# One decay table for all chunks, early loads in idle tiles, joined masks and a written-out order in a fused retention, spectral and gated MLP kernel

## The chip, the cores and the metric

The kernel runs on one core of one Trainium2 chip. The metric is the device time of one execution in microseconds (us). The kernel before takes 381.7 us, the median of 3 runs (381.68 to 381.8).

## The reference

Three stages follow one another. B is 2, there are 8 heads of 64 features, 768 tokens, and the model has 512 features; all data are float32.

```python
# 1: retention, a state per head that decays by gamma at every token
state = gamma * state + outer(k[t], v[t]);  y[t] = q[t] @ state / sqrt(64)
# 2: spectral mixing over tokens
theta = x @ w_theta
zr, zi = x * cos(theta), x * sin(theta)
u = x + w_tok_r @ zr + w_tok_i @ zi          # 768 x 768 over the tokens
x = u + relu(u @ w_ch)
# 3: gated MLP
h = gelu(x @ w_in);  hu, hv = halves of h
v_s = w_sg @ (layernorm(hv) * g_ln) + b_sg    # again over the tokens
out = x + (hu * v_s) @ w_out
```

## The kernel before

Each batch entry is cut into 6 chunks of 128 tokens, 12 chunks i in all. For a chunk, `retention(i)` (L432 on) loads q and k (`load_qk`, 512 KB), k and v (`load_kv`, 512 KB) and a table of q's decays (L485, 256 KB). TensorE then makes the scores, eight 64x128 products into two PSUM banks (`scores`). VectorE multiplies each bank by the causal mask (`mask`, L457, two instructions). ScalarE or VectorE scales v by its decay (`fade_v_heads`, eight instructions of L475, for the first 8 chunks; `fade_v`, L468, for the rest). TensorE makes k times v (`outer`), VectorE adds that to the state (`grow`, L507 and L509), and `attend` adds the state's part and the masked part into one bank. VectorE multiplies the result by the q decays into x (L554). Decays are counted from the start of the sequence, so each of the 6 chunk positions has a table of its own and the state itself is never scaled.

x lives in three tiles: `xa[0]`, `xa[1]` (the first four chunks of each batch entry) and `xb` (the last two of both). `theta(i)` multiplies x by w_theta, takes sine and cosine on ScalarE, turns x by four transposes with `ident` (L648) and multiplies (L656). `mix_main` and `mix_rest` do the token mixing. Then `channels`, `up_v`, `norm`, `up_u`, `gate_tile` and `finish` do the rest in 512-wide tiles.

Every wide product is exact to float32 by three passes of a two-part split: `split_hi` (L310, ScalarE) rounds a tile to float32r, `split_lo` (L316, VectorE) takes the remainder, and `terms3` (L290) issues high by high, low by high and high by low. The weights come packed in 64-bit words, 1 MB for each 128x1024 weight. `weight` loads one into a raw tile, unpacks it by L369 (ScalarE), L378 and L389 twice (VectorE), and splits it. There are two raw tiles (`RAWS`), so the third weight's load waits for the first's split.

The program is a list of operations, each for one engine with what it reads and writes (`Plan.op`). `Plan.schedule` gives them an order and buffers by estimated durations, due times (`prio`) and a look-ahead. The instructions stand on each engine in that order; what they wait for is found from the regions that they read and write. TensorE is kept busy before its data are there: eight products on a zeroed state (`warm`), and `keep_warm`, 128x128 products of `ident` with itself, which the schedule puts into gaps until a planned time of 34 us.

Of the kernel before, what the change touches and what calls it, by code (L numbers as in the profile page):

```python
# [18 lines left out]
P = 128  # L19
NCH = S // P  # L20
NP = H // 2
TA, TB = 512, 256
N = B * NCH

# [36 lines left out]
class Plan:  # L61
# [3 lines left out]
    BEGIN = {"PE": 5.2, "ACT": 2.0, "DVE": 2.0, "POOL": 1.3, "SP": 0.7}  # L65
# [28 lines left out]
    def schedule(self, look):  # L94


        engines = {o.eng: self.BEGIN.get(o.eng, 0.0) for o in self.ops}

        free = {of: [0.0] * n for of, n in self.room.items()}
        rank, level = {}, {}  # L100
        for k, o in enumerate(self.ops):
            o.missing, o.out = len(o.deps), []
            level[o] = max([o.lev, *(level[d] for d in o.deps)])
            rank[o] = k
            for d in o.deps:
                d.out.append(o)
        for o in self.ops:

            if o.eng == "SP" and o.out and not o.deps:
                level[o] = min(level[x] for x in o.out)  # L110
        for k, o in enumerate(sorted(self.ops, key=lambda o: (level[o], rank[o]))):
            o.pos = k
        use = {of: np.zeros(len(self.ops) + 1, np.int64) for of in self.room}
        for b in {b for o in self.ops for b in o.bufs}:
            b.todo = sorted(u.pos for u in b.users)
            b.first = b.todo[0]
            use[b.of][b.first : b.todo[-1] + 1] += 1
        for of, u in use.items():
            assert u.max() <= self.room[of], f"{of}: {u.max()} at {int(u.argmax())}"
        ready = {e: [] for e in engines}  # L120
        for o in self.ops:
            if not o.missing:
                ready[o.eng].append(o)
        state = {"port": 0.0, "dma": 2.1, "first": 0}
        done = [False] * (len(self.ops) + 1)

        def earliest(o):
            t = max(engines[o.eng], o.at, o.prio - (C["PA"] if o.eng == "PE" else C["AHEAD"]))
            if o.port:
                t = max(t, state["port"])  # L130
            o.spots = []
            more = {}
            for b in o.bufs:
                if b.base is not None:
                    continue
                n = more[b.of] = more.get(b.of, 0) + 1
                if b.first > state["first"]:
                    if use[b.of][state["first"] : b.first].max() + n > self.room[b.of]:
                        return None
                spots = sorted((x, k) for k, x in enumerate(free[b.of]) if x is not None)  # L140
                if len(spots) < n:
                    return None
                o.spots.append((b, spots[n - 1][1]))
                t = max(t, spots[n - 1][0] + self.LAT)
            return t

        for e in ready:
            for o in ready[e]:
                o.at = 0.0
        order = []  # L150
        while len(order) < len(self.ops):
            pick = None
            for e, ops in ready.items():
                at = [(t, o) for o in ops if (t := earliest(o)) is not None]
                if not at:
                    continue
                first = min(t for t, _ in at)
                t, o = min(
                    ((t, o) for t, o in at if t <= first + look.get(e, 0.0)),
                    key=lambda x: (x[1].until is not None, x[1].prio, x[0]),  # L160
                )
                if pick is None or t < pick[0]:
                    pick = (t, o)
            if pick is None:
                held = {e: len(v) for e, v in ready.items()}
                raise RuntimeError(f"no room: {len(order)} of {len(self.ops)}, {held}")
            t, o = pick
            earliest(o)
            if o.until is not None and t > o.until:
                o.dur, o.fn = 0.0, lambda: None  # L170
            ready[o.eng].remove(o)
            for b, b.base in o.spots:
                free[b.of][b.base] = None
                use[b.of][: b.first] += 1
            o.start = t
            engines[o.eng] = t + (0.45 if o.eng == "SP" else o.dur)
            if o.eng == "SP":
                state["dma"] = max(state["dma"], t + 0.45) + o.dur
                o.end = state["dma"] + 2.0
            else:  # L180
                o.end = t + o.dur
            if o.port:
                state["port"] = o.end
            done[o.pos] = True
            while done[state["first"]]:
                state["first"] += 1
            for b in o.bufs:
                last = b.todo[-1]
                b.todo.remove(o.pos)
                now = b.todo[-1] if b.todo else -1  # L190
                use[b.of][now + 1 : last + 1] -= 1
                if not b.todo:
                    free[b.of][b.base] = max(u.end for u in b.users)
            for x in o.out:
                x.missing -= 1
                if not x.missing:
                    x.at = max(d.end + (self.LAT if d.eng != x.eng else 0.0) for d in x.deps)
                    ready[x.eng].append(x)
            order.append(o)

        rank = {o: k for k, o in enumerate(order)}
        return sorted(order, key=lambda o: (o.start, rank[o]))


C = dict(TC=13, LATE=90, AHEAD=60, LM=28, LT=9, LR=16, LW=15, LRW=15, PEL=0.1, DVEL=0.1, ACTL=0.7, CHP=5, SGP=10, RW2=0, PA=25, DEL=6, RS=3.8, LEAD=40, TH=-8, WARM=34.0, NWARM=90, FA=8, LEAD1=5)
# [3 lines left out]
def retention_spectral_gmlp(  # L209
# [5 lines left out]
    dqs: bass.AP,  # L215
# [9 lines left out]
    nc.scalar.preload_act_table_set("silu_and_others")  # L225
# [16 lines left out]
    def bank():  # L242
        return Buf("psum")

    def halves(dtype=F32):
        b = Buf("pair", dtype)
# [59 lines left out]
    def dma(kb, fn, **k):  # L306
        return plan.op("SP", kb / 410.0, fn, **k)
# [799 lines left out]
    def keep_warm():  # L1107
# [3 lines left out]
        def products():  # L1111
            mm(ap(t)[:, 0:P], ident, ident, True, True)
# [87 lines left out]
```

## Time and profile before

| what | value |
|---|---|
| median of 3 runs | 381.7 us |
| the profiled execution: its span, first to last instruction | 381.1 us |
| TensorE busy | 374.7 us (98%), 2422 records |
| VectorE busy | 274.0 us (72%) |
| ScalarE busy | 175.0 us (46%) |
| GpSimd busy | 4.3 us (1%) |
| DMA | 41.96 MB, a mean of 110 GB/s |

The profiled execution is told by its span; the 0.6 us by which the median of the runs is longer lie around the first and the last instruction. The page's section on the chain of work that ended last puts 93% of the span on TensorE and 5% on the loads of q, k and v. A product of two float32 tiles leaves two matmul records in the trace, one of float32r tiles leaves one, so eight products of `scores` are "x16".

### The profile page before, as it was taken

Reading aid. Unit: us, or ns where it says so; the run is one execution under the profiler, and the core shown is the slowest. Engines: PE = TensorE matmul, PEld = TensorE weight load, DVE = VectorE, ACT = ScalarE, POOL = GpSimd, SP = SyncE. Lnnn points to the kernel's source line nnn. Section 1 sums busy time; section 2 is a strip of 40 time slices with the busy share of each in tenths; the row PEclk is TensorE's granted clock in tenths of the full one; section 3 lists DMA queues with packets and bytes.
Section 4 is the critical chain, followed back from the end, with each engine's and each line's share of the span. In section 5 each row is a group of like instructions: output and inputs, shape, how many; then the busy total and the mean of one; then the engine's idle time right before and its main releaser. Section 6 shows DMA issues by size and latency. Waiting matters only on the chain.

```text
span 381.1 us, 5873 instructions
## 1 busy us (share of the span) xinstructions
PE 374.7 (98%) x2422; PEld 318.4 (84%) x2422; DVE 274.0 (72%) x408; ACT 175.0 (46%) x292; POOL 4.3 (1%) x10
## 2 busy tenths in 40 slices
PE   7999999999999999999999999999999999999996
PEld 7877888878988978788998888888888888998885
DVE  1798999997977597869816685899899864544222
ACT  3677988563345335465313443595775711110000
POOL 1000000000000000003000000000000000000000
PEclk9999999999999999999999999999999999999999
DMA  7999553453435603029000160000000000000223
GB/s 258 411 407 407 208 191 110 144 223 132 165 114 192 248 2 113 0 101 352 4 2 2 31 244 2 1 0 0 2 0 1 2 1 0 2 2 35 103 89 106
DMA packets 11931, 41.96 MB, mean 110 GB/s; under 512 B 1536, under 2 KB 2560, under 8 KB 9472
## 3 DMA queue, kind: packets, MB, share of 16 engines
q1 hardware_dynamic: 11904, 41.58, 29.5%
q8 instruction: 19, 0.31, 0.3%
q14 instruction: 8, 0.07, 0.0%
HBM read 38.43 MB, written 3.15 MB: 109 GB/s over the span
## 4 chain that ended last, share of the span: by engine, by line
PE 93%; DMA 5%; SPq 0%; DVE 0%; issue 0%
PE b L290 92%; DMA b<-qkv 5%; PE b L648 1%; DVE b L1027 0%; SPq L424 0%; SPq L441 0%; SPq L413 0%
## 5 line engine op out<-in xcount | busy, mean ns | idle before, releaser
L290 PE MATMUL b<-b,b 128*128 128x512 f32 (+2 forms) x1788 | 332.6, 352 | 0.0
L290 PEld LDWEIGHTS b<-b,b 128*128 128x128 f32 (+1 forms) x1788 | 277.5, 183 | 47.0 <-issue 2.4
L310 ACT ACTIVATE b<-b 128x1024 fp32r<-128x1024 f32 (+1 forms) x64 | 53.2, 859 | 66.7 <-DVE b L975 38.2
L316 DVE TENSOR_TENSOR b<-b,b 128x1024 fp32r<-128x1024 f32 (+1 forms) x64 | 59.3, 955 | 9.7 <-ACT b L310 9.5
L389 DVE SCALAR_TENSOR_TENSOR b<-b 128x1024 int32<-128x1024 int32 x38 | 46.5, 1224 | 1.5 <-ACT b L369 0.5
L310 ACT ACTIVATE b<-xa 128x512 fp32r<-128x512 f32 x24 | 14.6, 626 | 22.9 <-DVE xa L777 9.9
L369 ACT ACTIVATE b<-b 128x1024 f32<-128x1024 f32 x19 | 21.8, 1155 | 3.6 <-DMA b<-wts 3.6
L290 PEld LDWEIGHTS b<-b 64*128 64x128 f32 (+1 forms) x352 | 17.3, 164 | 7.0 <-issue 2.8
L290 PE MATMUL b<-b 64*128 64x128 f32 (+1 forms) x352 | 20.5, 258 | 2.1 <-DMA b<-qkv 2.1
L457 DVE TENSOR_TENSOR b<-b,causal 128x512 f32<-128x512 f32 x24 | 15.7, 684 | 8.2 <-PE b L290 8.2
L316 DVE TENSOR_TENSOR b<-xa,b 128x512 fp32r<-128x512 f32 x24 | 16.2, 687 | 6.2 <-ACT b L310 6.0
L789 ACT ACTIVATE b<-b 128x512 f32<-128x512 f32 x24 | 13.8, 590 | 14.7 <-PE b L290 14.7
L475 ACT ACTIVATE b<-b,dk 128x64 f32<-128x64 f32 x64 | 16.1, 336 | 8.7 <-DMA b<-qkv 8.7
L968 DVE SCALAR_TENSOR_TENSOR b<-b,gcol,brow 128x512 f32<-128x512 f32 x12 | 9.0, 751 | 12.7 <-PE b L290 12.7
L813 DVE SCALAR_TENSOR_TENSOR b<-b,b 128x512 f32<-128x512 f32 x24 | 15.9, 678 | 2.9 <-ACT b L807 2.8
L807 ACT ACTIVATE b<-b 128x512 f32<-128x512 f32 x24 | 14.7, 629 | 6.2 <-DVE b L797 6.1
L797 DVE SCALAR_TENSOR_TENSOR b<-b,b 128x512 f32<-128x512 f32 x24 | 15.5, 672 | 1.9 <-ACT b L789 1.9
L604 ACT ACTIVATE b<-b 128x512 int32<-128x512 f32 x12 | 7.1, 594 | 19.9 <-PE b L290 19.9
L990 DVE TENSOR_TENSOR b<-b,xa 128x512 f32<-128x512 f32 x8 | 5.5, 690 | 14.2 <-PE b L290 14.2
L310 ACT ACTIVATE b<-xb 128x512 fp32r<-128x512 f32 x12 | 7.3, 628 | 17.5 <-DVE xb L735 9.9
L378 DVE TENSOR_SCALAR b<-b 128x1024 int32<-128x1024 int32 x19 | 13.1, 691 | 2.9 <-DMA b<-wts 2.7
L656 DVE TENSOR_TENSOR b<-b,b 128x1024 f32<-128x1024 f32 x12 | 14.6, 1220 | 0.8 <-ACT b L639 0.4
(51 smaller groups left out, 168.9 us busy)
## 6 DMA issues: line engine op xcount, KB each, us to landing
b<-wts SPq DMA_DIRECT2D x19, 1024.0 KB, 5.0
b<-qkv SPq DMA_DIRECT2D x24, 512.0 KB, 8.4
b<-dqs SPq DMA_DIRECT2D x12, 256.0 KB, 9.2
out<-b SPq DMA_DIRECT2D x11, 256.0 KB, 2.0
b<-wsg SPq DMA_DIRECT2D x9, 256.0 KB, 7.5
brow<-bvec SPq DMA_DIRECT2D x1, 384.0 KB, 7.7
out<-b SPq DMA_DIRECT2D x2, 128.0 KB, 1.7
dk<-decays SPq DMA_DIRECT2D x1, 24.0 KB, 3.4
```

Of the source, the lines that this page charges most:

```text
L290: nc.tensor.matmul(out=o, lhsT=l, rhs=r, start=start, stop=stop)
L310: act(words, lambda: A.activation(out=hi(), in_=src(), func=AF.Copy), prio=prio, r=r, **k)
L316: lambda: E.tensor_tensor(out=lo(), in0=src(), in1=hi().bitcast(F32), op=ALU.subtract),
L369: lambda: A.activation(out=words(1).bitcast(F32), in_=words(1).bitcast(F32), func=AF.Copy, scale=REBIAS),
L389: lambda scalar=scalar, op=op: V.scalar_tensor_tensor(out=words(0), in0=words(1), scalar=scalar, in1=words(0), op0=op, op1=ALU.bitwise_or,),
L457: V.tensor_tensor(out=ap(at[i])[:, h * 512 : (h + 1) * 512].rearrange("p (n t) -> p n t", n=NP), in0=ap(sc[h]).rearrange("p (n t) -> p n t ...
L475: A.activation(out=v, in_=v, func=AF.Copy, scale=dk[:, c, h : h + 1])
L656: V.tensor_tensor(out=z2, in0=ap(tp)[:, None, :].to_broadcast([P, 2, 512]), in1=z2, op=ALU.mult)
L789: lambda: A.activation(out=ap(s), in_=ap(t), func=AF.Square),
L797: lambda: V.scalar_tensor_tensor(out=ap(s), in0=ap(s), scalar=1.0 / GA, in1=ap(t), op0=ALU.add, op1=ALU.mult),
L807: lambda: A.activation(out=ap(s), in_=ap(s), func=AF.Tanh, scale=GA * GC),
L813: lambda: V.scalar_tensor_tensor(out=ap(o), in0=ap(s), scalar=1.0, in1=ap(t), op0=ALU.add, op1=ALU.mult),
```

## The change

It has seven parts.

- The decays are counted from the start of each chunk. One table `dec` (128x524, 262 KB) holds the q decays, the v decays and, per pair of heads, the decay of a whole chunk (`gone`). It is loaded once. The 12 loads of 256 KB (L485) and the 24 KB table `dk` go. In exchange the state is scaled by `gone` between chunks: in chunk 0 of a batch entry by VectorE, which now multiplies where it copied, and in chunks 1 to 4 by a GpSimd instruction (`shrink`, L522) between `grow` and the next chunk's `attend`.
- The two weights of theta land in `xb` and `xa[1]`, and a third weight in `xa[1]`, before these hold x. The two raw tiles are then free for others.
- The k and v of chunk 0 are loaded by a DMA that ScalarE issues; all others stay on SyncE. ScalarE's table load is issued behind it.
- The two masks of a chunk become one instruction over both banks. For that all of PSUM is one tile, `banks`, and the mask reads it with a stride from bank a to bank b.
- The scheduler's search is replaced by a list of 870 numbers, `ORDER`: the order in which operations are taken. Estimated times still set how each engine's instructions are merged.
- `keep_warm` products stand where the plan has a gap of TensorE of over 0.25 us, one per 0.24 us of gap.
- Some estimated durations in the plan are other numbers.

```diff
-    dk = const.tile([P, NCH, H], F32, name="dk")
+    dec = const.tile([P, 512 + H + NP], F32, name="dec")
+    dq, dk, gone = dec[:, 0:512], dec[:, 512 : 512 + H], dec[:, 512 + H :]
+    grown = const.tile([P, NP * D], F32, name="grown")
+    banks = psum.tile([P, 8 * 512], F32, tag="banks", name="banks")
...
-            b.tile = (psum if b.of == "psum" else const).tile(
-                [P, words[b.of]], b.dtype, tag=f"{b.of}{b.base}", name=f"b{len(tiles)}"
-            )
+            if b.of == "psum":
+                b.tile = banks[:, b.base * 512 : (b.base + 1) * 512]
...
+    homes = {
+        W_THETA: (xb.rearrange("p n b t -> p (n b t)"), [("x", b, c, d) for b in range(B) for c in (4, 5) for d in range(NP)]),
+        W_THETA + 1: (xa[1].rearrange("p n t -> p (n t)"), [("x", 1, c, d) for c in range(4) for d in range(NP)]),
+    }
+    homes[W_MAIN + 2] = homes[W_THETA + 1]
...
-            lambda: nc.sync.dma_start(out=ap(load[i, 1]), in_=qkv[b, c, 1]),
+            lambda: (nc.scalar if i == 0 else nc.sync).dma_start(
+                out=ap(load[i, 1]), in_=qkv[b, c, 1]
+            ),
...
-        for h in range(2):
-            def mask(h=h):
-                V.tensor_tensor(
-                    out=ap(at[i])[:, h * 512 : (h + 1) * 512].rearrange("p (n t) -> p n t", n=NP),
-                    in0=ap(sc[h]).rearrange("p (n t) -> p n t", n=NP),
-                    in1=causal[:, None, :].to_broadcast([P, NP, P]),
-                    op=ALU.mult,
-                )
-            dve(512, mask, ps=True, r=[sc[h]], w=[(at[i], h)], prio=t + 1)
+        def mask():
+            a, b = sorted(x.base for x in sc)
+            V.tensor_tensor(
+                out=ap(at[i]).rearrange("p (h n t) -> p h n t", h=2, n=NP),
+                in0=banks.rearrange("p (b n t) -> p b n t", b=8, n=NP)[:, a : b + 1 : b - a],
+                in1=causal[:, None, None, :].to_broadcast([P, 2, NP, P]),
+                op=ALU.mult,
+            )
+        dve(1024, mask, ps=True, r=sc, w=[at[i]], prio=t + 1)
...
                 if c == 0:
-                    V.tensor_copy(out=state_next, in_=add)
+                    V.tensor_tensor(out=state_next..., in0=add..., in1=gone..., op=ALU.mult)
                 else:
-                    V.tensor_tensor(out=state_next, in0=add, in1=state, op=ALU.add)
+                    V.tensor_tensor(out=grown, in0=add, in1=state, op=ALU.add)
+            def shrink():
+                G.tensor_tensor(out=state_next..., in0=grown..., in1=gone..., op=ALU.mult)
...
-    def keep_warm():
-        t = bank()
-        def products():
-            mm(ap(t)[:, 0:P], ident, ident, True, True)
-        plan.op("PE", 0.22, products, w=[t], prio=8.0, until=C["WARM"])
+    def keep_warm(bank, n):
+        for _ in range(n):
+            mm(banks[:, bank * 512 : bank * 512 + P], ident, ident, True, True)
+    for o in plan.schedule(ORDER):
+        if o.eng == "PE":
+            gap = o.start - done
+            if done < WARM and gap > 0.25:
+                ...
+                keep_warm(idle[0], int(gap / 0.24))
...
+ORDER = [
+    56, 57, 58, 84, 83, 0, 111, 110, 59, 60, 61, 87, 62, 64, 63, 85, 65, 137, 138, 66, 7, 75, 86,
...
```

The order on the engines moves in three places that matter below. An entry names the line, the operation and output<-inputs; "x8" is eight in a row.

The first place is TensorE's start. Before, the scores of chunk 0 (from b_96) are followed by 7 keep-warm products, the scores of chunk 1 (from b_101), and `outer` and `attend` of chunk 0; rows that only repeat are left out:

```order
L290 MATMUL warm<-state_81 128x128 x8
L290 MATMUL b_115<-ident 128x128
L290 MATMUL b_119<-b_96 128x128
L290 MATMUL b_129<-ident 128x128
L290 MATMUL b_154<-b_101 128x128
L290 MATMUL b_164<-b_99 64x64 x8
L290 MATMUL b_175<-b_131,b_99 64x128 x8
L290 MATMUL b_187<-ident 128x128
L290 MATMUL b_241<-b_107 64x64 x8
```

With the change it reads so, up to the first `attend` that reads a state scaled by GpSimd (chunk 2, from state_82, behind the scores of chunks 2 and 3 from b_108 and b_177):

```order
L282 MATMUL banks<-state_82 128x128 x8
L282 MATMUL banks<-b_96 128x128 x8
L282 MATMUL banks<-ident 128x128 x14
L282 MATMUL banks<-b_98 64x64 x8
L282 MATMUL banks<-b_118,b_98 64x128 x8
L282 MATMUL banks<-b_103 128x128 x8
L664 MATMUL banks<-ident,xa_85 128x128 x4
L282 MATMUL banks<-ident 128x128 x2
L282 MATMUL banks<-ident 128x128 x4
L282 MATMUL banks<-b_108 128x128 x8
L282 MATMUL banks<-b_177 128x128 x8
L282 MATMUL banks<-b_108,state_82 64x128 x8
```

All in all 29 keep-warm products stand before, 20 with the change, and the 14 behind the first scores are the longest run among these 20.

The second place is SyncE's first loads, before:

```order
L413 DMA b0_96<-qkv 128x1024
L441 DMA dk_80<-decays 128x48
L424 DMA b1_99<-qkv 128x1024
L413 DMA b2_101<-qkv 128x1024
L356 DMA b3_103<-wts 128x2048
L485 DMA b4_105<-dqs 128x512
```

and with the change, where b1_98, the k and v of chunk 0, is ScalarE's first instruction:

```order
L422 DMA b0_96<-qkv 128x1024
L453 DMA dec_80<-decays 128x524
L433 DMA b2_101<-qkv 128x1024
L422 DMA b3_103<-qkv 128x1024
L363 DMA xb_87<-wts 128x2048
L433 DMA b4_106<-qkv 128x1024
```

The third place is VectorE's masks in the second batch entry, and TensorE behind them. Before, two masks (of b_944 and b_946) stand on VectorE, and on TensorE 18 wide products follow the scores, none of which waits for these masks; the start of them is shown, with what each waits for:

```order
L290 MATMUL b_946<-b_532 128x128
L290 MATMUL b_955<-b_239,b_919 128x512 [waits Activation_49]
L290 MATMUL b_955<-b_239,b_919 128x512 [waits DVE_49]
L290 MATMUL b_955<-b_270,b_919 128x512
L457 TENSOR_TENSOR b_982<-b_944,causal 128x512 [waits DVE_49,PE_49]
L457 TENSOR_TENSOR b_982<-b_946,causal 128x512 [waits PE_49]
```

With the change, six wide products follow the scores (from b_604), and the next group has a wait for VectorE; further on, another group behind an `attend` has one, and the transposes behind that too. VectorE's rows at the two places stand last:

```order
L282 MATMUL banks<-b_604 128x128 x6
L282 MATMUL banks<-b_859,b_765 128x512
L282 MATMUL banks<-b_889,b_815 128x512 [waits DVE_49,Activation_49]
L282 MATMUL banks<-b_1235,b_1175 64x128 x7
L282 MATMUL banks<-b_619,b_1227 128x512 [waits DVE_49]
L664 MATMUL banks<-ident,xb 128x128 [waits DVE_49]
L470 TENSOR_TENSOR b_912<-banks,causal 128x1024 [waits PE_49]
L470 TENSOR_TENSOR b_1338<-banks,causal 128x1024 [waits PE_49]
L672 TENSOR_TENSOR b_1273<-banks,b_1273 128x1024 [waits Activation_49]
L570 TENSOR_TENSOR xb<-banks,dec 128x4x128
```

In the built program the number that the first waiting group waits for is the one that the mask of b_912 raises, the second group's is the mask of b_1338's, and the transposes' is that of the row of xb. The mask of b_912 reads banks 1 and 7 and waits for the six wide products before that group, which write bank 2; the mask of b_1338 reads banks 1 and 5 and waits for that `attend`, which writes bank 2. Of the twelve masks seven read neighbouring banks.

## Rows read from the trace of the kernel before

**Rows 1.** Page, busy time by engine and the chain that ended last.

```profile
PE 374.7 (98%) x2422; PEld 318.4 (84%) x2422; DVE 274.0 (72%) x408; ACT 175.0 (46%) x292; POOL 4.3 (1%) x10
PE 93%; DMA 5%; SPq 0%; DVE 0%; issue 0%
```

**Rows 2.** Chain in order of time: start us, us, what.

```profile
8.87 13.01 DMA b<-qkv
...
22.01 17.31 PE b L290 x216
...
169.25 208.88 PE b L290 x1068
```

**Rows 3.** Timeline of TensorE: start us, us, engine, line, operation [idle before].

```profile
1.26 3.60 PE L290 MATMUL warm<-state 128*128 128x128 f32 x16 [1.26 <-DVE state L269]
...
5.02 1.16 PE L290 MATMUL b<-b 64*128 64x128 f32 x16
6.11 1.83 PE L290 MATMUL b<-ident 128*128 128x128 f32 x14
8.99 1.78 PE L290 MATMUL b<-b 64*128 64x128 f32 x32 [1.04 <-DMA b<-qkv]
10.59 1.04 PE L290 MATMUL b<-b,b 128*64 128x128 f32 x16
11.57 4.06 PE L290 MATMUL b<-ident 128*128 128x128 f32 x34
15.56 0.69 PE L290 MATMUL b<-b 128*64 128x64 f32 x16
16.18 1.09 PE L290 MATMUL b<-b,state 64*64 64x128 f32 x16
...
18.78 1.16 PE L290 MATMUL b<-b 64*128 64x128 f32 x16 [0.49 <-DMA b<-qkv]
19.88 0.66 PE L648 MATMUL b<-ident,xa 128*128 128x128 f32 x4
20.37 1.06 PE L290 MATMUL b<-ident 128*128 128x128 f32 x8
22.01 1.78 PE L290 MATMUL b<-b 64*128 64x128 f32 x32 [0.59 <-DMA b<-qkv]
```

**Rows 4.** SyncE's two DMAs in hand from 1.1 to 1.3 us: KB each, us from issue to landing.

```profile
b<-qkv SPq DMA_DIRECT2D x1, 512.0 KB, 3.4
dk<-decays SPq DMA_DIRECT2D x1, 24.0 KB, 3.4
```

**Rows 5.** Stretches of 1 us: busy by engine, PEclk, DMA share, GB/s.

```profile
1.00:2.00 1.00, 0.74 (x3) 0.74 (x4) 0.21 (x1) 1.00 (x1) 0.73 (x3) 1.00 0.32 49
2.00:3.00 1.00, 1.00 (x7) 1.00 (x6) 0.00 (x0) 0.06 (x1) 0.00 (x0) 1.00 0.86 324
3.00:4.00 1.00, 1.00 (x7) 1.00 (x7) 0.00 (x0) 0.00 (x0) 0.00 (x0) 1.00 0.87 220
4.00:5.00 1.00, 1.00 (x7) 0.90 (x6) 0.00 (x0) 0.00 (x0) 0.00 (x0) 1.00 0.88 169
5.00:6.00 1.00, 1.00 (x17) 0.97 (x16) 0.00 (x0) 0.00 (x0) 0.00 (x0) 1.00 0.89 287
10.00:22.00 12.00, 10.93 (x146) 9.81 (x143) 9.98 (x13) 7.35 (x18) 0.00 (x0) 1.00 1.02 408
```

**Rows 6.** Timeline, window 84 to 91 us, VectorE and TensorE.

```profile
83.33 1.22 DVE L316 TENSOR_TENSOR b<-b,b 128x1024 fp32r<-128x1024 f32 x1
...
84.46 0.69 DVE L468 TENSOR_TENSOR b<-b,dk 128x512 f32<-128x512 f32 x1
...
86.32 4.38 PE L290 MATMUL b<-b,b 128*128 128x512 f32 x18
87.34 1.28 DVE L457 TENSOR_TENSOR b<-b,causal 128x512 f32<-128x512 f32 x2
```

**Rows 7.** Page, costliest groups: xcount | busy us, mean ns of one | idle before.

```profile
L656 DVE TENSOR_TENSOR b<-b,b 128x1024 f32<-128x1024 f32 x12 | 14.6, 1220 | 0.8 <-ACT b L639 0.4
```

**Rows 8.** Timeline of GpSimd, 160 to 186 us.

```profile
177.46 1.22 POOL L1085 TENSOR_SCALAR gcol<-gcol 128x4 f32<-128x4 f32 x1 [175.60 <-DMA gcol<-gvec]
178.09 2.54 POOL L1086 TENSOR_SCALAR brow<-brow 128x768 f32<-128x768 f32 x1
```

**Rows 9.** Timeline of VectorE, theta weight's unpacking and the state's sum.

```profile
17.38 0.70 DVE L378 TENSOR_SCALAR b<-b 128x1024 int32<-128x1024 int32 x1 [1.67 <-DMA b<-wts]
17.99 0.42 DVE L509 TENSOR_TENSOR state<-b,state 128x256 f32<-128x256 f32 x1
...
19.46 2.48 DVE L389 SCALAR_TENSOR_TENSOR b<-b 128x1024 int32<-128x1024 int32 x2
21.86 0.68 DVE L316 TENSOR_TENSOR b<-xa,b 128x512 fp32r<-128x512 f32 x1
```

More of the change, by code (lines that the diff above doesn't have):

```diff
@@ L23 @@
 N = B * NCH
+WARM = 34.0
 INV2PI = 1.0 / (2.0 * math.pi)
@@ L92, in op, with schedule @@
         return o
-    def schedule(self, look):
-        engines = {o.eng: self.BEGIN.get(o.eng, 0.0) for o in self.ops}
+    def schedule(self, order):
+        engines = dict(self.BEGIN)
         free = {of: [0.0] * n for of, n in self.room.items()}
[L100 to L106, printed above, removed]
-        for o in self.ops:
[L109 to L128, printed above, removed]
@@ L129, in earliest @@
+        todo = {}
+        for o in self.ops:
+            for b in o.bufs:
+                todo[b] = todo.get(b, 0) + 1
+        port = sent = skew = 0.0
+        landed, last = [], {}
+        for o in (self.ops[k] for k in order):
+            t = max([engines[o.eng], *(d.end + (self.LAT if d.eng != o.eng else 0.0) for d in o.deps)])
             if o.port:
-                t = max(t, state["port"])
-            o.spots = []
-            more = {}
+                t = max(t, port)
+            if o.eng == "SP" and len(landed) >= self.FLY:
+                t = max(t, landed[-self.FLY])
@@ L133, in earliest @@
             for b in o.bufs:
[L134 to L160, printed above, removed]
-                )
[L162 to L174, printed above, removed]
-            o.start = t
[L176 to L179, printed above, removed]
@@ new lines, in schedule @@
+                if b.base is None:
+                    room = free[b.of]
+                    b.base = min(range(len(room)), key=lambda k: room[k])
+                    if room[b.base]:
+                        t = max(t, room[b.base] + self.LAT)
+                    room[b.base] = math.inf
+            o.start = t
+            if o.eng in ("SP", "SPA"):
+                engines[o.eng] = t + 0.45
+                if sent < t + 1.0:
+                    sent, skew = t + 1.4, 0.3
+                sent += o.dur
+                skew = min(2.8, skew + 0.25 * o.dur)
+                o.end = sent + skew
+                if o.eng == "SP":
+                    landed.append(o.end)
@@ L180, in schedule @@
             else:
-                o.end = t + o.dur
+                engines[o.eng] = o.end = t + o.dur
             if o.port:
[L183 to L186, printed above, removed]
+                port = o.end
             for b in o.bufs:
[L188 to L205, printed above, removed]
+                todo[b] -= 1
@@ new lines, in schedule @@
+                last[b] = max(last.get(b, 0.0), o.end)
+                if not todo[b]:
+                    free[b.of][b.base] = last[b]
+        assert math.inf not in [x for room in free.values() for x in room]
+        rank = {k: n for n, k in enumerate(order)}
+        return [self.ops[k] for k in sorted(order, key=lambda k: (self.ops[k].start, rank[k]))]
+C = dict(TC=13.26, LATE=79.43, AHEAD=65.28, LM=28.32, LT=9.09, LR=20.66, LW=14.3, LRW=7.12, PEL=0.1, DVEL=0.06, ACTL=0.83, CHP=38.15, SGP=4.68, RW2=0, PA=37.2, DEL=5.73, RS=2.59, LEAD=38.54, TH=-5.54, WARM=33.56, NWARM=90, FA=8, LEAD1=6.04)
@@ L1179 @@
     )
-    dqs, dk = _decays()
     arrays = {
```

125 lines of the change are left out of this document (75 added, 50 removed), and 44 rows, old and new, of the table ORDER.

## Prediction

> **What bounds the kernel now.** I read the page's busy times first: TensorE is busy for 98% of the span, VectorE for 72%, GpSimd for almost nothing, and the chain that ended last lies 93% on TensorE and 5% on DMAs [rows 1]. Where those 5% are, the chain in order of time tells: after 22.01 us it runs on TensorE in unbroken stretches, the last from 169.25 to 378.13, behind which only a last VectorE instruction and the store of the output follow [rows 2]. So the time is three things in a row: what is lost ahead of 22.01, TensorE's own work, and a tail of 3.0 us (381.1 − 378.1). The change leaves the number and shape of the real products as they are, and the tail; VectorE, ScalarE and the DMAs matter only where TensorE would wait for them.
>
> What is lost ahead of 22.01 I add up from TensorE's timeline [rows 3], where it is not on a product of q, k, v or x: 5.02 us to the first scores; 6.11 to 8.99 (keep-warm, then a wait for k and v), 2.88; 11.57 to 15.56 (keep-warm), 3.99; the wait of 0.49 before 18.78; 20.37 to 22.01, 1.64. Together **14.0 us**; the other 8.0 are work. The 17 keep-warm products of the second gap (34 records, 3.99 us) give 0.235 us for one.
>
> **Part by part.**
>
> *Start.* TensorE must wait only for q and k of chunk 0. They land 3.4 us after their issue at 0.79 [rows 4], at 4.2, inside the products on the zero state, which end at 1.26 + 3.60 = 4.86 [rows 3]. The change puts more bytes beside that load: ScalarE issues k and v of chunk 0 at the start, and the table behind it is 262 KB, not 24. If loads did not delay one another, the first scores would start at 4.8, the lower end. For the other end the seconds at which DMAs ran slowly count: from 1 to 6 us 49, 324, 220, 169 and 287 GB/s went, 1.05 MB in all [rows 5], which is what both 512 KB loads need; if both share alike at these rates, both land at 6.0, and the scores start some 0.6 us later (from landing to start, 5.02 − 4.2 is 0.8 at most), at **6.6**. The dip to 169 stands where the 24 KB table goes, which takes 3.4 us as the 512 KB do [rows 4]; its rows are small pieces, and in the new table they are ten times as long. At the full 408 GB/s of 10 to 22 us [rows 5], 1.05 MB would be there by about 4.5, and the start at 5.1. I take 5.5, nearer to that row, since the table that went with the dip is gone.
>
> The Trainium skill ("DMA: Bandwidth & Descriptors", section "Issuing engines are not separate DMA queues") says that transfers issued by different engines run interleaved on the same 16 DMA engines, and that a second issuer saves issue time only. That speaks against the early k and v; with it the sum is the one below, without it the one of rival B.
>
> *Keep-warm.* Of 29 products 20 are left, 14 of them behind the first scores; they are issued whether there is a gap or not. 20 × 0.235 = **4.7 us** [rows 3]. They also stand for the waits: 14 are 3.3 us, in which k and v of chunk 0 land. Behind them no wait for a load is left in my sum: the early chunks' loads lose the 256 KB tables between them, 12 tables in all, 3.1 MB or 7.6 us at 408 GB/s [rows 5].
>
> *Masks.* Two instructions of 128x512 (1.28 us both [rows 6]) become one of 128x1024, at the price of the other 128x1024 instructions that read PSUM, 1.22 us [rows 7]. VectorE gains 0.06 per chunk, covered by its idle 28%. The new thing is a wait. The order shows two groups of wide products with a wait for VectorE, which is the mask's: a mask over banks 1 and 7, or 1 and 5, is taken to read all that lies between, so it waits for the products ahead that write bank 2, and the next group that writes a bank in between waits for it. Before, 18 wide products ran beside two masks, with no wait [rows 6]. Each place costs TensorE 0.1 us until the mask starts, 1.22 of mask [rows 7] and 0.1 until the next product: about 1.4, twice, 2.85. Behind the second place the transposes wait for VectorE, which has the theta sum (1.22, spaced 1.13 as its like are [rows 6]) and x times the decays (0.69) to do behind the mask, while TensorE has only one group of six, 1.5 us: about 0.4 more. Together **3.3 us**. The bounds are 0, if the wait did not bind, and 3 × 1.4 + 0.4 = 4.6, if a third mask bound too; I take what the order shows.
>
> *Shrink.* One GpSimd instruction for each of eight chunks, 128x256 with two inputs. No row has one. The nearest are of 128x4, 1.22 us, the first of its kind, and of 128x768, 2.54 [rows 8]; the line between them gives 1.65. What decides is the first one, ahead of chunk 2's `attend`. TensorE comes there after four scores (1.16 twice, 1.78 for two), three times `outer` (0.69), three halves of `attend` (1.04 to 1.09) and four transposes (0.66), 10.0 us [rows 3], and the 4.7 of keep-warm: at 5.5 + 14.7 = 20.2. VectorE comes to the sum ahead of the shrink like this: scores of chunk 1 end at 5.5 + 1.16 + 3.3 + 0.69 + 1.04 + 1.16 = 12.85, then mask 1.13, remainder of x 0.60, unpacking 0.61 and 2.48, sum 0.42 [rows 6, 9], with 0.1 ahead of the mask: 18.2. So the shrink is hidden up to 2.0 us. At 1.65 it costs nothing.
>
> *The rest.* Weights in idle x tiles, ScalarE's table load behind a DMA, chunk 0's copy that becomes a product: VectorE and ScalarE have the room [rows 1], and after 22.01 TensorE waits for none of them [rows 2]. Cost 0; if their cover were gone, the first theta products would wait, which the slack of the shrink's chain (2.0 us) would take first.
>
> **Sum.** 381.1 − 14.0 + 5.5 + 4.7 + 3.3 = 380.6 against the profiled span; the median lies 0.6 above that span, so **381.2 us**, −0.5 or −0.13%. A measurement of this kernel can tell about 0.2% (0.76 us) from no change, so this is "the same": the start gives 3.8 us, the masks take 3.3. Its own range, with the start from 5.0 to 6.3, is 380.7 to 382.0. Chance 0.41.
>
> **Rivals.**
> - *B: the loads don't delay each other.* For it: with two loads and the small table under way, the rate was far under 408 [rows 5], so there is room. Against: in 2 to 5 us the DMA share was 0.86 to 0.88, little idle. First scores at 4.8: 380.5. Chance 0.25.
> - *C: the mask waits don't bind.* The change then does all that it can: 381.2 − 3.3 = 377.9. Against it stand the waits in the order and the lack of any gap in TensorE's chain to put them into. Chance 0.08.
> - *D: both first loads at the slow rate*, scores at 6.6: 382.3. For it: the rate of 169 [rows 5]; against it: the small-piece table is gone. Chance 0.10.
> - *E, slower: GpSimd becomes the bound* at chunk 2's `attend`. It decides from 2.0 us on, each further us is one lost. A price of 2.54 gives 381.7; with a first call's 1.22 on top, 3.76 [rows 8], it gives 381.2 + 1.8 = 383.0. For it: 4 columns already took 1.22; a start later than 5.5 shifts both sides alike and heals nothing. Against it: a third of 768 columns. Chance 0.16.
>
> The Trainium skill ("GPSIMD Engine Reference", section "2.1 Instruction dispatch") states that the first call of freshly loaded GpSimd code pays about 6 us. If this held for the first shrink, the estimate from that page is some 4 us above the forecast, near 385.5. The first GpSimd call of another kind, in [rows 8], shows no such price with its 1.22, so I give it no more than a part of E's chance.
>
> **How the numbers follow.** Faster: B, C and a sliver of the forecast (start before 5.2), 0.25 + 0.08 + 0.05 = 0.38. Slower: E and the far edge of the forecast, 0.16 + 0.02 = 0.18. Same: the forecast's rest and D, 0.34 + 0.10 = 0.44. The range goes from 380.0 (B with a start at 4.8 and masks 0.5 cheaper) to 383.1 (E): it leaves out C and the end of E, some 0.15.
>
> **What would show it.** TensorE's timeline: first scores at 5.5 (4.8 is B, 6.6 is D); then 14 keep-warm products for 3.3 us, and `outer` of chunk 0 without a wait. In the table of waits: two of TensorE for VectorE's mask line, each about 1.4 us, and one of 0.4 for x; without them C holds. The shrink's rows on GpSimd near 1.65 us, and no wait of TensorE for POOL ahead of chunk 2's `attend`; a wait there is E. The last product should end at about 377.6, and TensorE's waits after 22 us sum to 3.3. The forecast is wrong if that sum is under 1 or over 5, if the first scores come outside 4.8 to 6.6, or if TensorE waits for theta's weights.

## The result and the profile after

The changed kernel takes **384.1 us**, the median of 5 runs (383.49 to 384.13); the kernel before took 381.68 in the same session (381.58 to 381.8). The ratio is 1.0053 with a 95% interval of 1.0037 to 1.0069: slower by half a per cent. The forecast was 381.2 in a range of 380.0 to 383.1, with 0.18 for slower.

| | before | after |
|---|---|---|
| median | 381.7 us | 384.1 us |
| span of the profiled execution | 381.1 us | 382.4 us |
| spans of timed runs | 379.6 to 381.3 us (39 runs, median 380.0 to 380.1 in each of three sessions) | 381.8 to 382.4 us (5 runs) |
| time minus span, in those runs | 1.7 us | 1.7 us |

The prediction did not have the last two rows. In every timed run, of either kernel, the time is 1.7 us longer than the span, to within 0.1. So the 0.6 us that the text ahead of the prediction puts around the first and the last instruction is not what lies there: by this the profiled execution of before, with its span of 381.1, was itself 1.1 us longer than the median, though its own time is not on record. It is no rarity: 9 of the 39 timed runs have spans of 380.6 or more, all of them in the second and the third session.

The page after, busy times and the chain that ended last:

```profile
PE 374.5 (98%) x2404; PEld 317.2 (83%) x2404; DVE 269.9 (71%) x396; ACT 173.6 (45%) x292; POOL 15.1 (4%) x18
PE 97%; DMA 1%; DVE 1%; issue 0%
```

The chain's share of DMAs fell from 5% [rows 1] to 1%, and TensorE is still the bound. TensorE's timeline to chunk 2's `attend` (start, length, what), the part that answers to [rows 3]:

```profile
1.26 3.78 PE L282 MATMUL banks<-state 128*128 128x128 f32 x16 [1.26 <-DVE state L261]
5.51 1.91 PE L282 MATMUL banks<-b 64*128 64x128 f32 x16 [0.47 <-DMA b<-qkv]
7.35 3.39 PE L282 MATMUL banks<-ident 128*128 128x128 f32 x28
10.67 0.69 PE L282 MATMUL banks<-b 128*64 128x64 f32 x16
...
14.45 0.71 PE L282 MATMUL banks<-ident 128*128 128x128 f32 x4
...
17.14 1.16 PE L282 MATMUL banks<-ident 128*128 128x128 f32 x8
18.23 2.87 PE L282 MATMUL banks<-b 64*128 64x128 f32 x48
21.02 1.09 PE L282 MATMUL banks<-b,state 64*64 64x128 f32 x16
```

The first scores start at 5.51, as forecast, but after a pause of 0.47 us, and they fill 1.84 us (from their start to the next row's, 5.51 to 7.35) where they filled 1.09 in [rows 3] (5.02 to 6.11). The keep-warm products fill 3.32 us (to 10.67), 0.64 (to 15.09, the next row left out) and 1.09: 5.05. Chunk 2's `attend` waits for nothing.

From the table of waits, over the whole span (us in total, times, longest; PEld is TensorE's weight load):

```profile
PE banks L282 <- DVE b L470: 2.7, 2, 1.4
...
PEld banks L664 <- DVE xb L570: 0.5, 1, 0.5
PE banks L282 <- DMA b<-qkv: 0.5, 1, 0.5
```

And the chain in order of time, at these two waits and at the end:

```profile
89.52 1.24 DVE b L470
...
90.89 1.62 PE banks L282 x6
...
139.79 1.23 DVE b L470
141.02 1.13 DVE b L672
142.15 0.61 DVE xb L570
...
142.80 0.66 PE banks L664 x4
...
160.62 218.47 PE banks L282 x1110
```

There they are: the mask of the joined banks (L470) twice, and behind the second one the theta sum (L672) and x times the decays (L570), for which the transposes' first weight load waits 0.5 us. TensorE's products themselves show no third wait. The last product ends at 160.62 + 218.47 = 379.1, against 378.13 in [rows 2], and 3.3 us of tail follow.

The shrinks on GpSimd, two of the eight:

```profile
18.82 0.61 POOL L522 TENSOR_TENSOR state<-grown,dec 128x256 f32<-128x256 f32 x1 [16.95 <-DMA xa<-wts]
...
51.13 4.33 POOL L522 TENSOR_TENSOR state<-grown,dec 128x256 f32<-128x256 f32 x1 [17.80 <-DVE grown L519]
```

The first took 0.61 us and ended at 19.4, 1.6 before TensorE came for it. The eight together take 11.7 us, 1.46 in the mean.

### The profile page after: what moved, and what is told of

Its sections match the earlier page's. It is cut to its first block, busy times and chain, and to the rows that moved or that the text cites. A ratio compares the mean times of both kernels' runs of the same rounds, so it can differ in the third digit from the quotient of the medians.

```text
span 382.4 us, 5777 instructions
## 1 busy us (share of the span) xinstructions
PE 374.5 (98%) x2404; PEld 317.2 (83%) x2404; DVE 269.9 (71%) x396; ACT 173.6 (45%) x292; POOL 15.1 (4%) x18
## 4 chain that ended last, share of the span: by engine, by line
PE 97%; DMA 1%; DVE 1%; issue 0%
PE banks L282 95%; PE banks L664 2%; DMA b<-qkv 1%; DVE b L470 1%; DVE b L672 0%; DVE xb L570 0%; DVE b L1043 0%
## 5 line engine op out<-in xcount | busy, mean ns | idle before, releaser
L282 PE MATMUL banks<-b,b 128*128 128x512 f32 (+2 forms) x1788 | 332.9, 352 | 2.7 <-DVE b L470 2.7
L282 PEld LDWEIGHTS banks<-b,b 128*128 128x128 f32 (+1 forms) x1788 | 277.6, 183 | 50.7 <-issue 4.2
L302 ACT ACTIVATE b<-b 128x512 fp32r<-128x512 f32 (+1 forms) x61 | 50.6, 847 | 84.1 <-DVE b L394 31.6
L308 DVE TENSOR_TENSOR b<-b,b 128x512 fp32r<-128x512 f32 (+1 forms) x61 | 56.3, 939 | 12.5 <-ACT b L302 11.1
L470 DVE TENSOR_TENSOR b<-banks,causal 128x1024 f32<-128x1024 f32 x12 | 14.7, 1222 | 15.4 <-PE banks L282 15.3
L813 DVE SCALAR_TENSOR_TENSOR b<-b,banks 128x512 f32<-128x512 f32 x24 | 16.1, 684 | 13.4 <-ACT b L805 13.4
L302 ACT ACTIVATE b<-xa 128x512 fp32r<-128x512 f32 (+1 forms) x26 | 16.9, 666 | 18.8 <-DVE xa L793 7.8
L282 PEld LDWEIGHTS banks<-b 64*128 64x128 f32 (+1 forms) x352 | 17.9, 170 | 5.3 <-issue 2.7
L282 PE MATMUL banks<-b 64*128 64x128 f32 (+1 forms) x352 | 21.2, 264 | 0.5 <-DMA b<-qkv 0.5
L308 DVE TENSOR_TENSOR b<-xa,b 128x512 fp32r<-128x512 f32 (+1 forms) x26 | 19.2, 742 | 0.4 <-ACT b L302 0.2
L829 DVE SCALAR_TENSOR_TENSOR b<-b,banks 128x512 f32<-128x512 f32 x24 | 16.2, 682 | 4.2 <-ACT b L823 2.4
L488 ACT ACTIVATE b<-b,dec 128x64 f32<-128x64 f32 x64 | 16.0, 337 | 3.9 <-DMA dec<-decays 3.9
L522 POOL TENSOR_TENSOR state<-grown,dec 128x256 f32<-128x256 f32 x8 | 11.7, 1458 | 113.8 <-DVE grown L519 96.9
L672 DVE TENSOR_TENSOR b<-banks,b 128x1024 f32<-128x1024 f32 x12 | 14.6, 1218 | 1.2 <-ACT b L647 1.1
```

The lines of the kernel that those rows point to most:

```text
L282: nc.tensor.matmul(out=o, lhsT=l, rhs=r, start=start, stop=stop)
L302: act(words, lambda: A.activation(out=hi(), in_=src(), func=AF.Copy), prio=prio, r=r, **k)
L308: lambda: E.tensor_tensor(out=lo(), in0=src(), in1=hi().bitcast(F32), op=ALU.subtract),
L470: V.tensor_tensor(out=ap(at[i]).rearrange("p (h n t) -> p h n t", h=2, n=NP), in0=banks.rearrange("p (b n t) -> p b n t", b=8, n=NP)[:, a ...
L488: A.activation(out=v, in_=v, func=AF.Copy, scale=dk[:, h : h + 1])
L672: V.tensor_tensor(out=z2, in0=ap(tp)[:, None, :].to_broadcast([P, 2, 512]), in1=z2, op=ALU.mult)
```

## Experiments

There are eleven runs, one of them the kernel before once more. One reading serves in nearly all of them: how long it is from the start of chunk 0's `outer` (the row 128x64 x16 behind the first keep-warm group) to the end of the last product. In the changed kernel it is 379.10 − 10.67 = 368.43. It separates what happens at the start from everything behind it. The kernel before, in these sessions, had medians of 381.72, 381.82 and 381.85.

**1. The k and v of chunk 0 on SyncE.**

```diff
-            lambda: (nc.scalar if i == 0 else nc.sync).dma_start(
+            lambda: nc.sync.dma_start(
```

> The changed kernel with k and v of chunk 0 issued by SyncE, second behind q and k, so that ScalarE issues no DMA. Theory (the queue of ScalarE costs time outside the span: 384.1 against a span of 382.4 is 1.7, before it was 0.6): time minus span falls from 1.7 to 0.6, and the time from 384.1 to about 383.0. Rival (the 1.1 us outside belong to something else, GpSimd or the PSUM tile): time minus span stays 1.7. Inside the span both expect little: the table of decays is issued 0.5 later, its fades and so the first outer are hidden behind 14 keep-warm products; first scores start between 5.0 and 5.6.

Measured: 383.33 (383.03 to 383.55), span 381.4 in the profiled run, time minus span 1.7 to 1.8 in every run. So the theory of time outside the span is refuted: taking the early load from ScalarE's queue changes nothing there, and the spans of the kernel before, listed with these runs, show the same 1.7. What the edit gave lies inside the span:

```profile
4.98 1.25 PE L282 MATMUL banks<-b 64*128 64x128 f32 x16
6.15 3.39 PE L282 MATMUL banks<-ident 128*128 128x128 f32 x28
9.47 0.69 PE L282 MATMUL banks<-b 128*64 128x64 f32 x16
```

First scores at 4.98 with no pause, `outer` at 9.47, 1.20 earlier; the last product ends at 377.89, 1.21 earlier (distance 368.42). In the median the gain is 0.8. The DMA issues at 0.7 to 1.0 us of the changed kernel, and then of this one, tell why (KB, us to landing):

```profile
b<-qkv ACTq DMA_DIRECT2D x1, 512.0 KB, 4.9
b<-qkv SPq DMA_DIRECT2D x1, 512.0 KB, 4.7
```

```profile
b<-qkv SPq DMA_DIRECT2D x1, 512.0 KB, 3.3
```

Issued at the same moment by two engines, the two loads of chunk 0 take 4.7 and 4.9 us; behind each other on SyncE, q and k take 3.3, as in [rows 4]. That is what the Trainium skill's rule says ("DMA: Bandwidth & Descriptors", "Issuing engines are not separate DMA queues"): they share the same engines. A second load issued in the same moment makes the load that is waited for 1.4 us later than one issued 0.4 us behind it; a second issuer with a later start was not tried.

**2. The shrink on VectorE.**

```diff
-                G.tensor_tensor(
+                V.tensor_tensor(
                     out=state_next.rearrange("p (n d) -> p n d", n=NP),
```

> The changed kernel with the eight shrinks on VectorE in place of GpSimd. Theory (the shrink is hidden, and the time outside the span is not GpSimd's): 384.1 within 0.3, time minus span stays 1.7; eight more VectorE instructions of about 0.4 us, all covered. Rival (GpSimd's code or its slow rows, up to 4.3 us, cost time): 0.5 to 1.1 us less.

Measured: 384.77 in the median, but on two levels: 383.40 and 384.01, 385.54 and 385.84. The profiled run is one of the upper:

```profile
5.65 2.08 PE L282 MATMUL banks<-b 64*128 64x128 f32 x16 [0.61 <-DMA b<-qkv]
7.67 4.83 PE L282 MATMUL banks<-ident 128*128 128x128 f32 x28
12.42 0.69 PE L282 MATMUL banks<-b 128*64 128x64 f32 x16
```

Its last product ends at 380.85, which is 368.43 behind `outer`, as in the changed kernel. So in these two profiles it makes no difference to what follows where the shrink runs: the eight instructions of 0.42 us on VectorE are as well hidden as GpSimd's. The 1.75 us more lie ahead of 12.42, in products that have nothing to do with the shrink; the next two runs show what that is. The two lower times, 383.40 and 384.01, are the changed kernel's (383.49 to 384.13) within 0.1.

**3. The masks split again.**

```diff
-            a, b = sorted(x.base for x in sc)
-            V.tensor_tensor(... in0=banks...[:, a : b + 1 : b - a] ...)
+            for h in range(2):
+                V.tensor_tensor(
+                    out=ap(at[i])[:, h * 512 : (h + 1) * 512]...,
+                    in0=ap(sorted(sc, key=lambda x: x.base)[h])...,
+                    in1=causal[:, None, :].to_broadcast([P, NP, P]),
+                    op=ALU.mult,
+                )
```

> The changed kernel with two mask instructions per chunk, one for each bank, in the same place of the same order. Theory (the two waits of TensorE for the joined mask, 2.7 us, and a bit behind the second, come from the banks between): both waits go, 384.1 - 3.0 = 381.1. Rival (the wait is real, VectorE is late there in any case, or TensorE meets another wait right behind): less than 1 us is gained.

Measured: 382.14 in the median of ten, on two levels again: seven runs of 382.01 to 382.38, three of 379.95 to 380.24. TensorE's waits for VectorE's masks are gone from the table; 12 wide products run beside the two masks:

```profile
89.43 3.04 PE L282 MATMUL banks<-b,b 128*128 128x512 f32 x12
89.74 1.28 DVE L470 TENSOR_TENSOR b<-banks,causal 128x512 f32<-128x512 f32 x2
```

The profiled run is one of the upper level; its `outer` starts at 12.27 and its last product ends at 377.32. That is 365.05, where it was 368.43: **the joined masks cost 3.38 us**. Record by record, the changed kernel falls behind this run by 1.6 us at the first waiting group, by 1.5 more at the second and by 0.3 more at the transposes. The median hides it because the start took 1.6 us longer in the profiled run, and, by their times, in the six others of the upper level:

```profile
5.56 2.08 PE L282 MATMUL banks<-b 64*128 64x128 f32 x16 [0.52 <-DMA b<-qkv]
7.57 4.77 PE L282 MATMUL banks<-ident 128*128 128x128 f32 x28
```

The same 28 records of keep-warm took 3.39 us in the changed kernel's profile. The stretch from 8 to 9 us shows it, in this run and in the changed kernel (busy time and instructions of TensorE first, the granted clock third from the end):

```profile
8.00:9.00 1.00, 1.00 (x6) 1.00 (x6) 1.00 (x2) 1.00 (x5) 0.00 (x0) 1.00 1.09 455
```

```profile
8.00:9.00 1.00, 1.00 (x11) 1.00 (x10) 0.77 (x1) 1.00 (x5) 0.00 (x0) 1.00 1.09 455
```

Six records of the same product in one microsecond, or eleven: TensorE goes at half its rate in the first. The granted clock reads 1.00, the upper level of 2.4 GHz, in both rows, but in the first that is no reading: the column counts time that no clock record covers as 1.00, and this trace's first clock record, of the upper level, begins at 10.49 us. In the changed kernel's trace it begins at 7.11. Ahead of these moments only the spacing of records tells the rate, and it halves just there, so the recorded clock and the records agree. The Trainium skill ("TensorE: Matmul & The Clock Gate", "Seeing it yourself") warns that recorded clock events have been seen to be unreliable; no run here shows it.

**4. Ten products at the start.**

```diff
-    for _ in range(8):
+    for _ in range(10):
         mm(warm[:, 0:P], states[0][:, 0:P], states[0][:, 0:P], True, True)
```

> The changed kernel with ten products on the zero state at the start in place of eight, so that TensorE has no pause ahead of the first scores. Theory (the pause of 0.47 us keeps TensorE at half its rate for the first scores, 1.91 us where they took 1.16 before): first scores start at 5.5 as before, take about 1.2, and 0.7 us is gained: 383.4. Rival (the first scores are slow because of the load that has just landed, or TensorE speeds up at a fixed time): they still take 1.9 and nothing is gained, or the extra products push them back by 0.4.

Measured: 383.52 (383.40 to 383.74), one level.

```profile
5.60 1.16 PE L282 MATMUL banks<-b 64*128 64x128 f32 x16
6.70 3.39 PE L282 MATMUL banks<-ident 128*128 128x128 f32 x28
10.02 0.69 PE L282 MATMUL banks<-b 128*64 128x64 f32 x16
```

With no pause the first scores fill 1.10 us in place of 1.84, `outer` starts 0.65 earlier, and the last product ends 0.65 earlier. The load that has just landed is not the cause: it took 4.8 us here too. Nor does TensorE speed up at a fixed time. By the traces' first clock records it reached the upper level between 4.6 and 7.0 us in the ten profiles with no pause ahead of the first scores (4.6 in the profiled execution of before, 5.0 in this run, 5.2 in run 1), and in the three with one at 7.1 (the changed kernel), 10.5 and 10.7 (runs 3 and 2). So the pause goes with a later moment, but how much of the 0.75 us is the pause's in the one profile of the changed kernel is not shown: with no pause, the first scores filled 1.51 us in run 6 and 1.82 in run 8.

**5. Ten products at the start, no keep-warm.**

```diff
-WARM = 34.0
+WARM = 0.0
```

> Ten products on the zero state, and none of the 20 keep-warm products behind them. Against the run with ten and all keep-warm products, 383.5. Theory (the 14 behind the first scores stand there whether TensorE would wait or not: the first outer could start when v is decayed, about 8.6, and started at 10.0): 1.4 to 3 us less, 380.5 to 382.1. Rival (in the pauses that take their place TensorE falls back to half its rate, and what follows runs slowly): no gain, 383.5 or more.

Measured: 380.46 (380.23 to 380.97), 3.06 below run 4, at the upper end of what the theory allowed. The 20 products, 5.05 us, gave 3.06. Of the rest, a part came back because TensorE reached its upper level later in this profile (6.8 us, for 5.0 in run 4), and a part where `outer` follows the decay of v head by head; the two were not separated. From 6.8 us on the granted clock is 1.00 throughout, so the rival falls.

```profile
5.83 2.96 PE L282 MATMUL banks<-b 64*128 64x128 f32 x32
8.84 1.09 PE L282 MATMUL banks<-b,b 128*64 128x128 f32 x16
```

(Scores and `outer` of chunk 0 are one row here.) Chunk 0's `attend` starts at 8.84, where it started at 10.53 in run 4.

**6. Split masks and ten products.** The edits of runs 3 and 4 together.

> Split masks and ten products on the zero state. The split masks alone gave 382.1 in the median, with single runs near 382.2 and near 380.1. Theory (the two levels come from the pause ahead of the first scores, behind which TensorE runs at half its rate for 2 us in some executions and 6 us in others; without the pause there is only one): all runs near 379.5, within 0.4. Rival (the two levels have another cause): both levels remain, near 381.5 and 379.5.

Measured: 380.64 in the median of seven (379.90 to 381.04), higher than either level of the theory, but without the level near 382.2. The distance is 365.04 again. In the profiled run the ten products lasted until 5.9 at half rate, TensorE changed at 6.7, within the first scores (1.51 us), and `outer` started at 10.66. So taking the pause away removes the worst of it: of the 24 executions of experiments 1, 4, 5, 6 and 7, whose profiles show no pause ahead of the first scores, none lies more than 1.2 us above the fastest of its kernel; of the 19 of the changed kernel and experiments 2 and 3, whose profiles show one, 9 stand on an upper level, 1.5 us or more above every run of the lower. It does not remove the spread of about 1 us.

**7. Split masks and k and v of chunk 0 on SyncE.** The edits of runs 3 and 1 together.

> Split masks, and k and v of chunk 0 issued by SyncE. Theory (ScalarE's early issue delays q and k by 0.5 us and so makes the pause; the gains add): 383.3 - 3.4 = 379.9, one level. Rival (the load on SyncE pushes the others back, and with the mask waits gone TensorE then waits for data): 381 or more.

Measured: 379.62 (379.44 to 380.32), against 379.9 expected: ratio to before 0.9944, interval 0.9928 to 0.9961. The gains add; `outer` starts at 9.41, and the last product ends 365.05 later.

**8. The kernel before, profiled again.** No edit.

> The kernel before, profiled once more. The timed runs of it have spans of 379.6 to 380.3 and times 1.7 longer; the profiled execution that the prediction rests on had a span of 381.1. Theory (that execution was 1.1 us longer than most, in the waits for the first loads): span near 380.0, and the waits ahead of the unbroken stretch some 1.1 us shorter. Rival (its length is usual): span 381.1.

Measured: 381.84, span 380.1, the median of the timed runs.

```profile
5.40 1.88 PE L290 MATMUL b<-b 64*128 64x128 f32 x16
7.22 1.83 PE L290 MATMUL b<-ident 128*128 128x128 f32 x14
9.16 1.78 PE L290 MATMUL b<-b 64*128 64x128 f32 x32
...
19.98 1.06 PE L290 MATMUL b<-ident 128*128 128x128 f32 x8
20.97 1.78 PE L290 MATMUL b<-b 64*128 64x128 f32 x32
```

TensorE waits for no load here; the page's waits for loads were 2.1 us in the execution that the prediction read (its longest in [rows 3]: 1.04, 0.49, 0.59). The unbroken stretch starts at 20.97 in place of 22.01, and ends at 377.12 in place of 378.13. The load that the scores at 18.78 of [rows 3] waited for took 13.7 us from its issue and landed at 18.7; here its like took 11.8 and landed at 17.2. So 1.0 of the 1.1 us by which that execution was longer were late loads. TensorE reached its full rate late in this one, at 7.0: the first scores fill 1.82 us. It costs nothing here, because the scores of chunk 1 could not have started before 9 us anyway; in [rows 3], with the change at 4.6, a wait of 1.04 stands in its place.

**9. Split masks, k and v on SyncE, no keep-warm.** Experiment 7 with the edit of WARM to 0.0.

> Split masks, k and v of chunk 0 issued by SyncE, and no keep-warm product, with the eight products at the start. Theory (the three gains add): the run with the first two gave 379.6; without keep-warm the same 3.0 less as in the run without it, 376.6. Rival 1 (with first scores done at 6.1, TensorE waits for the decay of v until 6.4 and longer, and part of the 3.0 comes back as waits): 377 to 378. Rival 2 (in that wait TensorE falls to half its rate, as it did in the pause of the changed kernel): some executions 2 us longer.

Measured: 377.54 (377.38 to 379.04), ratio to before 0.9876, interval 0.9858 to 0.9893. Both rivals show: the median lies in the first one's range, and the profile, which is of the longest execution, shows the second:

```profile
4.98 1.16 PE L282 MATMUL banks<-b 64*128 64x128 f32 x16
8.31 2.04 PE L282 MATMUL banks<-b 128*64 128x64 f32 x15 [2.17 <-ACT b L488]
...
10.25 1.82 PE L282 MATMUL banks<-b,b 128*64 128x128 f32 x15
12.00 1.16 PE L282 MATMUL banks<-b 64*128 64x128 f32 x16
```

TensorE waits 2.17 us for the decay of v, which begins at 7.9, when the table of decays has landed, and began at 6.4 in run 4. The 15 records of `attend` that take 1.0 at full rate elsewhere take 1.82. Here the clock column does show it (third from the end; 0.50 is the lower level, 1.2 GHz):

```profile
9.00:10.00 1.00, 1.00 (x12) 1.00 (x11) 0.00 (x0) 1.00 (x5) 0.00 (x0) 0.50 1.02 426
```

The trace's record has the upper level from 5.0, the lower from 8.4 and the upper again from 11.8. So TensorE fell from full rate in this wait; in the pause of the changed kernel, which the expectation likens to it, it had not yet reached it. Chunk 2's `attend` waits 0.16 us for the shrink in this run: with 5 us of products gone, that shrink is no longer quite hidden.

**10. Split masks, ten products, no keep-warm.** Experiment 6 with the edit of WARM to 0.0.

> Split masks, ten products at the start, no keep-warm product, k and v of chunk 0 issued by ScalarE as in the change. Theory (what delays the first scores, ScalarE's early issue, no longer matters once VectorE and ScalarE's work on v is what TensorE waits for): 380.5 - 3.4 = 377.1, within 0.5 of the run with SyncE's issue. Rival (the early issue costs here too): 0.5 or more above that run.

Measured: **377.36** (376.72 to 377.84), ratio to before 0.9868, interval 0.9849 to 0.9887: faster than both kernels, by 4.5 and 6.7 us, and 0.2 from experiment 9, within the spread of both. Which engine issues k and v makes no difference that these runs can tell. TensorE now waits for loads again, a little:

```profile
14.29 1.78 PE L282 MATMUL banks<-b 64*128 64x128 f32 x32 [0.25 <-DMA b<-qkv]
16.68 1.16 PE L282 MATMUL banks<-b 64*128 64x128 f32 x16 [0.62 <-DMA b<-qkv]
```

**11. The kernel before without keep-warm.**

```diff
         def products():
-            mm(ap(t)[:, 0:P], ident, ident, True, True)
+            pass
```

> The kernel before without its 29 keep-warm products, all else as it is. Theory (before, the products filled real waits, for loads and for theta's weights, that the change has shortened): less than 1 us is gained, 380.9 to 381.8. Rival (they stood in TensorE's way as they do in the changed kernel): 2 us or more are gained, 379.7 or less. Third: TensorE falls to half its rate in the waits, and it is slower, 383 or more.

Measured: 381.72 (381.18 to 383.83), no difference (ratio 0.9994, interval 0.9978 to 1.0010): the theory, though one of the ten runs took 383.83. Where the products were, TensorE waits for loads:

```profile
4.97 1.69 PE L290 MATMUL b<-b 64*128 64x128 f32 x16
9.46 3.09 PE L290 MATMUL b<-b 64*128 64x128 f32 x32 [2.79 <-DMA b<-qkv]
12.33 1.35 PE L290 MATMUL b<-b,b 128*64 128x128 f32 x16
14.27 2.00 PE L290 MATMUL b<-b 128*64 128x64 f32 x16 [0.58 <-DVE b L457]
```

It falls to half its rate in these waits, too (two chunks' scores in 2.87 us, 9.46 to 12.33, for 1.60 in [rows 3]; the granted clock is 0.50 from 9.54 to 12.95), with the same end, 377.0 for 377.1 in experiment 8.

## Why the prediction was wrong

Forecast −0.5 us, measured +2.4: 2.9 us lie between them, 1.1 ahead of the sum and 1.8 inside it. Either alone would have left the time inside the range; both together did not.

- **The first step that failed: the median stands 0.6 above the profiled span.** The sum, 380.6 of span, was put against an execution that was 1.1 us longer than the median of the kernel before, because loads came late in it; the 14.0 us "lost ahead of 22.01" held 1.0 us of that. By the median span, 380.0 or 380.1, and the 1.7 us around it, the same sum gives 382.3: no gain, and just short of "slower". This line alone turns the sign of the forecast.
- **The second: the first scores as unchanged work.** Their start at 5.5 came out, at 5.51, and with it the mechanism: the two loads delay each other. That it came out to 0.01 is luck, since 5.5 was chosen between 5.1 and 6.6. But the scores filled 1.84 us, not 1.09: **+0.75**, because TensorE was still at half its rate until 7.1. The part on the start took them at full rate, as if that came at a fixed time. [rows 3] held the sign of it: 16 records on the zero state fill 3.60 us, 34 of keep-warm, a product of the same size, 4.06.
- **Keep-warm at 0.235 each, 4.7 us: 5.05 measured, +0.35.** The price came from a row of 17; in the groups of two and four one takes 0.32 and 0.27. That the products would stand in the way at all, since the waits they filled were gone, is in no rival; experiment 5 gives it as 3.06.
- **Masks, 3.3 us: 3.38 by experiment 3.** Right in place, mechanism and size, two waits of 1.4 and the transposes behind the second; +0.1.
- **Shrink, hidden at an estimated 1.65 us: hidden, at 0.61 for the first.** Rival E falls with it; experiment 2 moves nothing behind the start. The line drawn through [rows 8] is near the mean of the eight, 1.46, but they range from 0.61 to 4.33, and a call of 4.33 at the first one's place would have ended 2.1 us after TensorE came. So that the short ones stood there was in part luck. E had the right sign, slower, by a mechanism that did not act. The 385.5 named beside it is by its own terms, 381.2 and 4, 385.2.
- **The tail, taken as unchanged: 3.3 us for 3.0, +0.3.** The last 0.3 us of the 1.8 lie in TensorE's work itself. By the spacing of records they are the transposes': these take 5.3 us in experiment 7, 5.0 in experiment 8, while the other real products of the two agree within 0.2 where both run at full rate. Why a transpose is dearer in the new order was not tried.
- **Rival B** (loads don't delay each other) is refuted by the DMA rows of experiment 1, 4.7 us against 3.3; **C** by the waits in the table; **D** by the start. The rate of 169 GB/s in [rows 5] did not come back, as the prediction reckoned.

The change removes what it says it removes: with the masks split, two more products at the start and no keep-warm it is 4.5 us faster than before (experiment 10). The kernel before gets nothing from dropping its keep-warm products (experiment 11), since TensorE then waits 3.7 us for loads. What the change saved at the start it paid out again: 3.1 us of products that stood for waits no longer there, 3.4 us of joined masks.

## What to carry to other kernels

Profile a kernel twice before a forecast of a fraction of a per cent is hung on its span, and compare the span with those of the timed runs: an execution whose first loads came late carries waits that the median does not have. When a change shortens a wait, look at what was put there to fill it; a fixed number of filler products costs time once the wait is gone, here 3.06 us of their 5.05. An instruction that reads two pieces of one large tile with a stride may be taken to read everything between them, and its waits then show in the order of instructions before anything runs.

## What was not expected of the hardware

- The moment at which TensorE reaches its full rate differs from execution to execution of the same program: at 4.6 us in one profiled execution of the kernel before and 7.0 in another, with no pause in either and the same products from 1.26 us on. With a pause of 0.5 to 0.6 us ahead of the first scores it came at 7.1, 10.5 and 10.7. The column of the granted clock reads 1.00 ahead of that moment because no clock record stands there. Why it comes when it does stays open.
- A two-input GpSimd instruction of 128x256 took from 0.61 to 4.33 us in one run, the 4.33 while VectorE worked without a gap, and 0.93 in experiment 1 at the same place of the program. The Trainium skill ("GPSIMD Engine Reference", "Key points") states that the two engines share their ways to SBUF; whether that is the cause was not tried. The Trainium skill ("GPSIMD Engine Reference", "2.1 Instruction dispatch") gives 6 us for the first call of freshly loaded code; this does not show: the first shrink took 0.61 and began 0.1 us after VectorE's sum had ended.
